# Two loads of v moved from SyncE's queue to ScalarE's, in sparse attention with a max-out layer behind it

## The chip, the cores and the metric

The kernel runs on one core of one Trainium2 chip. The metric is the device time of one execution in microseconds. The engines are TensorE (PE), VectorE (DVE), ScalarE (ACT), GpSimd (POOL) and SyncE (SP, which here only issues transfers). The 16 DMA engines of the core move the data; loads are issued from SP's queue (q1 in the profile), the stores of the output mostly from ScalarE's (q10).

## The reference

Two stages. The first is attention over 4 batches, 8 heads, 768 positions of 64 elements: each position sees the positions less than 16 away, and a summary of every block of 32 positions. The summary of k is the block's maximum, that of v its mean.

```
k_sum = k.reshape(B, H, nb, block, D).max(axis=3)          # block 32, nb 24
v_sum = v.reshape(B, H, nb, block, D).mean(axis=3)
scores_l = where(|i - j| < 16, scale * q @ k.T, -1e9)
scores_s = scale * q @ k_sum.T + log(32)
a = softmax(concat([scores_l, scores_s]))
x = (a @ concat([v, v_sum]))          # heads side by side: 3072 tokens x 512
```

The second stage is a feed-forward layer of 1,024 hidden units that takes the larger of two products:

```
out = maximum(x @ w1, x @ w2) @ w_out
```

## The kernel before

**Tiling.** The work on attention goes by batch b (0 to 3) and by pair of heads hp (0 to 3). In the text k12 is k of batch 1, pair 2; likewise q and v. k and q of a pair are loaded in 32-bit floats (384 KB each, `load_kq`, L358), cast to 16 bits (`prep`, L515), turned by TensorE (or, in some pairs of later batches, by a DMA) and placed in SBUF; the block maxima of k are put beside k. v of a pair is loaded by `load_v` (L371, also 384 KB, in 1,536 pieces of 256 B), cast by `cast_v` (L384) and spread by `spread_v` (L392): copies to the odd tiles, block sums by TensorE (L432), and copies of the sums. `scores` (L582) multiplies q and k, with an exponential on ScalarE (L625) behind it; `values` (L635) multiplies by v, VectorE divides (L659, L661), and the result is turned (L674) into xt.

The max-out layer uses max(a, b) = a + max(b - a, 0). `load_w12` (L688) loads w1 and w2 in two halves each (four loads of 1 MB) and makes the difference wd (L700, two on GpSimd and two on VectorE). `load_wo` (L724) loads w_out, `make_w1o` (L733) computes w1 times w_out, so that the layer is x (w1 w_out) + max(x wd, 0) w_out. `maxout` (L749) makes the hidden products (L757), the Relu (L762) and the output (L778, L785).

**Order of the work.** Every piece of work is handed to a planner (`Plan`, L113) as a task with an engine, an estimated duration, the buffers it reads and writes, and a priority. The planner simulates the engines and fixes one order of all tasks, by its own estimates; `run` (L155) then calls the tasks' functions in that order, which issues the instructions. On the chip each engine works through its instructions strictly in that order and waits by semaphores for what it needs. In the planned order SP issues, in batch 0: k00, q00, v00, k01, q01, v01, k02, q02, k03, q03, v02, v03, then the four weight loads, then q10, k10, v10, k11, q11 and the two loads of w_out. ScalarE has: cast k00, cast q00, two small copies of k00, cast v00, exp of pair 0 (first part), place k01, exp of pair 0 (second part), the odd copies of v01 and its sums, cast k03, two small copies of k01, place q03, exp of pair 1, cast v03 and so on. On GpSimd stand cast q01, cast q02, cast q03, the copies of the sums of v01, cast v02. The cast of v00 is planned directly behind the load of q03 in the overall order.

**Buffers and semaphores.** There are four buffers for loaded v (`vfr`, L247), six for k and q, four for weights, so that w_out needs buffers that the first halves of w1 and w2 held. The loads take eight completion semaphores in turn, and the issue of a load waits until the earlier load with the same semaphore has landed. With the order given above, v02 shares a semaphore with v00, and v03 with k01.

**Fillers.** `stay_busy` (L823) puts 40 tasks of two products of zeros (L830) among TensorE's first work, where it would otherwise be idle.

Of the kernel before, what the change touches and what calls it, by code (L numbers as in the profile page):

```python
# [16 lines left out]
ACT = mybir.ActivationFunctionType  # L17
# [64 lines left out]
class Task:  # L82
    done, start = 1e9, None
# [29 lines left out]
class Plan:  # L113
# [9 lines left out]
    def op(self, engine, us, fn, read=(), write=(), change=(), touch=(), behind=(), prio=0.0, label="", port=False):  # L123
        t = Task()
        t.engine, t.us, t.fn, t.label = engine, us, fn, label
        t.port = engine == "POOL" or port and engine == "DVE"
        t.prio = (prio + CFG["bump"].get(label, 0), len(self.tasks))
        t.new, t.behind = [*write, *change], behind
        t.deps = {w for b in (*read, *change) for w in b.writers}
        for b in t.new:  # L130
            b.writers.append(t)
        for b in (*read, *touch, *t.new):
            b.users.append(t)
        self.tasks.append(t)
        return t
# [57 lines left out]
def kernel(  # L193
# [14 lines left out]
    nc = tc.nc  # L208
    B, H, S, D = 4, 8, 768, 64
# [10 lines left out]
    op = plan.op  # L220
# [39 lines left out]
    vx = [Buf(vxr) for _ in range(B)]  # L260
# [109 lines left out]

    def load_v(b, hp, prio):  # L371
        f = vin[b, hp] = Buf(vfr)
        op("SP", 1.9, lambda: nc.sync.dma_start(  # L373
            out=f.ap[:].rearrange("p h m d -> p (h m) d"),
            in_=v[b, 2 * hp:2 * hp + 2].rearrange("h (m r) d -> r (h m) d", r=128)),
           write=[f], prio=prio, label=f"load v{b}{hp}")

    def by_parity(b):
        return vx[b].ap[:].rearrange("p (m w) h c -> p w m h c", w=2)

    vin, mains = {}, {}
    ready = {(b, hp): Buf(Ring([None])) for b in range(B) for hp in range(NP)}

    def cast_v(b, hp, engine, prio):  # L384

        f, done = vin[b, hp], Buf(Ring([None]))
        mains[b, hp] = done
        copy(engine, {"D": 0.6, "A": 0.85, "P": 0.8}, lambda: (
            by_parity(b)[:, 0, :, 2 * hp:2 * hp + 2, 0:D].rearrange("p m h d -> p h m d"), f.ap[:]),
             read=[f], write=[vx[b], done, ready[b, hp]], prio=prio, label=f"cast v{b}{hp}")  # L390

    def spread_v(b, h0, h1, prio, engines):  # L392

# [91 lines left out]
    def copy(engine, us, aps, label, port=True, halves=False, **kw):  # L485
        engine = ENG[engine]
        us = us if isinstance(us, float) else us[engine[0]]
        def fn():
            for o, i in [aps(0), aps(1)] if halves else [aps()]:
                {"DVE": nc.vector.tensor_copy, "ACT": nc.scalar.copy,  # L490
                 "POOL": nc.gpsimd.tensor_copy}[engine](out=o, in_=i)
        op(engine, us, fn, label=label, port=port, **kw)
# [354 lines left out]
    for hp in range(NP):  # L847
        load_kq(0, hp, hp)
        load_v(0, hp, CFG["kv"][hp])
        cast_v(0, hp, CFG["vc"][hp], CFG["kv"][hp])  # L850
        spread_v(0, 2 * hp, 2 * hp + 2, CFG["kv"][hp] + CFG["sp"], (CFG["od"][hp], CFG["se"][hp], CFG["sr"][hp]))
# [5 lines left out]
    for b in range(1, B):  # L857
        for hp in range(NP):
            at = 1000 * b + 20 * hp - CFG["ld"]
            load_kq(b, hp, at)  # L860
            load_v(b, hp, at + 10)
            cast_v(b, hp, CFG["lvc"][4 * b - 4 + hp], at + 10)
        spread_v(b, 0, H, at + 11, (CFG["lod"][b - 1], CFG["lse"][b - 1], CFG["lsr"][b - 1]))
        attention(b, 1000 * b)
# [37 lines left out]
```

## Time and profile before

| what | value |
|---|---|
| three runs | 172.28, 170.13, 171.58 us; median 171.58 |
| the profiled execution | 172.63 us, of which the span of the trace is 170.9 us |
| instructions | 4,532 |
| mean granted TensorE clock | 0.999 |
| read from HBM, written | 25.17 MB, 6.29 MB |
| DMA, mean over the span | 210 GB/s |
| q1 (SP's loads and turns), q10 (ScalarE's stores) | 73.1% and 10.6% of the 16 engines' time |

The largest shares of the chain of work that ended last are TensorE 64%, DMA 13%, the SP queue 10% and VectorE 8%. In a timeline, each row has the start, the duration, the engine (a q behind it marks an instruction that its sequencer handles, such as the issue of a DMA), the line, the operation, what it writes and reads, and in brackets the idle time ahead of it with what ended it. Rows of the same kind that follow each other are merged and carry their number (x3). Casts and copies that one helper issues all stand under L490. Times are microseconds from the start of the span.

### The profile page before, as it was taken

Reading aid. Unit: us, or ns where it says so; the run is one execution under the profiler, and the core shown is the slowest. Engines: PE = TensorE matmul, PEld = TensorE weight load, DVE = VectorE, ACT = ScalarE, POOL = GpSimd, SP = SyncE. Lnnn points to the kernel's source line nnn. Section 1 sums busy time; section 2 is a strip of 40 time slices with the busy share of each in tenths; the row PEclk is TensorE's granted clock in tenths of the full one; section 3 lists DMA queues with packets and bytes.
Section 4 is the critical chain, followed back from the end, with each engine's and each line's share of the span. In section 5 each row is a group of like instructions: output and inputs, shape, how many; then the busy total and the mean of one; then the engine's idle time right before and its main releaser. Section 6 shows DMA issues by size and latency. Waiting matters only on the chain.

```text
span 170.9 us, 4532 instructions
## 1 busy us (share of the span) xinstructions
PE 159.0 (93%) x1859; PEld 106.5 (62%) x1859; DVE 105.7 (62%) x224; ACT 93.0 (54%) x146; POOL 42.2 (25%) x73
## 2 busy tenths in 40 slices
PE   4885598999899999999999999999999999999992
PEld 4765366998546555568475675775746658756662
DVE  6778999899678998547996562929628460000001
ACT  3667485486963456626167476491665706523420
POOL 7713789340227041009200201104110000000000
PEclk9999999999999999999999999999999999999999
DMA  5999799999999999998499999993864617011113
GB/s 176 307 310 282 186 395 380 332 320 360 274 315 227 218 307 317 229 190 231 90 223 333 261 273 174 252 158 74 190 151 112 145 35 184 4 61 62 61 61 123
DMA packets 69396, 35.82 MB, mean 210 GB/s; under 512 B 56576, under 2 KB 63360, under 8 KB 69376
## 3 DMA queue, kind: packets, MB, share of 16 engines
q1 hardware_dynamic: 65856, 29.38, 73.1%
q10 hardware_dynamic: 3520, 6.16, 10.6%
q8 instruction: 14, 0.23, 0.6%
q14 instruction: 6, 0.05, 0.1%
HBM read 25.17 MB, written 6.29 MB: 184 GB/s over the span
## 4 chain that ended last, share of the span: by engine, by line
PE 64%; DMA 13%; SPq 10%; DVE 8%; issue 2%; POOL 1%; DVEq 0%; POOLq 0%
PE banks L785 22%; PE banks L757 19%; PE banks L778 10%; DMA wf<-in_moe_w_dram 8%; DMA wf<-in_moe_w_out_dram 5%; SPq L367 5%; PE banks L741 4%; PE banks L648 3%; SPq L373 3%; DVE vx L490 3%; PE banks L600 3%; SPq L693 3%; PE banks L543 1%; DVE ks L562 1%; DVE qx L490 1%
## 5 line engine op out<-in xcount | busy, mean ns | idle before, releaser
L785 PE MATMUL banks<-wo,g 128*128 128x512 bf16 (+2 forms) x208 | 46.9, 363 | 0.0
L757 PE MATMUL banks<-xt,wd 128*128 128x256 bf16 x384 | 46.4, 273 | 0.0
L757 PEld LDWEIGHTS <-wd 128*128 128x128 bf16 x384 | 36.7, 98 | 6.5 <-issue 0.2
L762 ACT ACTIVATE g<-banks 128x512 bf16<-128x512 f32 x48 | 27.8, 602 | 13.7 <-PE banks L757 13.5
L794 ACT COPY o<-banks 128x512 f32<-128x512 f32 x23 | 13.5, 587 | 32.4 <-PE banks L785 30.8
L785 PEld LDWEIGHTS <-g 128*128 128x128 bf16 x208 | 18.4, 98 | 17.7 <-issue 0.2
L778 PE MATMUL banks<-w1o,xt 128*128 128x512 bf16 (+2 forms) x104 | 23.7, 363 | 0.0
L490 POOL CAST kqb<-kqf 128x768 bf16<-128x768 f32 x12 | 11.6, 968 | 37.1 <-PE banks L543 17.4
L625 ACT ACTIVATE pba<-banks 128x1024 bf16<-128x1024 f32 x16 | 16.4, 1025 | 6.2 <-PE banks L600 5.7
L632 DVE TENSOR_TENSOR pba<-pba,mask 128x1024 bf16<-128x1024 bf16 x12 | 8.5, 711 | 14.1 <-ACT pba L625 14.1
L490 DVE COPY o<-banks 128x128 f32<-128x128 f32 x2 | 0.6, 292 | 26.8 <-PE banks L785 26.8
L661 DVE TENSOR_TENSOR xs<-banks,inv 128x512 bf16<-128x512 f32 x24 | 16.3, 687 | 0.6
L562 DVE TENSOR_REDUCE ks<-kx 128x24 bf16<-128x768 bf16 x16 | 15.0, 945 | 1.3 <-DMA kx<-kqb 1.2
L778 PEld LDWEIGHTS <-xt 128*128 128x128 bf16 x104 | 9.8, 98 | 8.8
L490 POOL CAST vx<-vf 128x768 bf16<-128x768 f32 x7 | 6.2, 889 | 23.4 <-DMA vf<-in_v_dram 23.3
L600 PEld LDWEIGHTS <-kx 64*128 64x128 bf16 x416 | 7.3, 96 | 6.7 <-issue 5.7
L490 ACT CAST kqb<-kqf 128x768 bf16<-128x768 f32 x9 | 7.9, 880 | 5.6 <-DMA kqf<-in_k_dram 2.7
L625 ACT ACTIVATE pbb<-banks 128x512 bf16<-128x512 f32 x16 | 9.7, 604 | 0.9 <-ACT o L794 0.9
L830 PE MATMUL banks<-zeros 128*128 128x128 bf16 x80 | 8.5, 259 | 1.8 <-DVE zeros L826 1.8
L490 POOL COPY kx<-kx 128x32 bf16<-128x32 bf16 (+1 forms) x12 | 5.5, 462 | 18.3 <-DMA kx<-kqb 12.1
L490 DVE COPY vx<-vx 64x3168 bf16<-64x3168 bf16 (+5 forms) x15 | 9.3, 632 | 0.2
L600 PE MATMUL banks<-qx,kx 64*128 64x64 bf16 (+2 forms) x416 | 9.4, 190 | 0.0
(85 smaller groups left out, 188.3 us busy)
## 6 DMA issues: line engine op xcount, KB each, us to landing
kqf<-in_k_dram SPq DMA_DIRECT2D x16, 384.0 KB, 6.7
kqf<-in_q_dram SPq DMA_DIRECT2D x16, 384.0 KB, 5.8
vf<-in_v_dram SPq DMA_DIRECT2D x16, 384.0 KB, 7.5
out_dram<-o ACTq DMA_DIRECT2D x19, 256.0 KB, 3.2
wf<-in_moe_w_dram SPq DMA_DIRECT2D x4, 1024.0 KB, 9.6
wf<-in_moe_w_out_dram SPq DMA_DIRECT2D x2, 1024.0 KB, 9.3
out_dram<-o ACTq DMA_DIRECT2D x4, 224.0 KB, 3.2
vx<-sums SPq DMA_DIRECT2D x4, 99.0 KB, 3.3
```

Of the source, the lines that this page charges most:

```text
L367: op("SP", (1.2, 1.13)[n], lambda f=f, src=src: nc.sync.dma_start(out=f.ap[:], in_=src[b, 2 * hp:2 * hp + 2].rearrange("h (p j) d -> p h ( ...
L490: {"DVE": nc.vector.tensor_copy, "ACT": nc.scalar.copy, "POOL": nc.gpsimd.tensor_copy}[engine](out=o, in_=i)
L562: op("DVE", 0.95, lambda: nc.vector.tensor_reduce(out=ks.ap[:], in_=free(kt(), 128, [256, NM], [192, 2], [32, 2], [1, 32]), axis=AX.X, op= ...
L600: nc.tensor.matmul(out=bank(ps[i], 1024)[:, 512 * a + at + n0:512 * a + at + n1], lhsT=kx[b, hp].ap[r, 128 * t + 128:128 * t + 256], rhs=q ...
L625: op("ACT", (1.03, 0.6)[i], lambda: nc.scalar.activation(out=pv(), in_=bank(ps, 1024).rearrange("p (a c) -> p a c", a=2)[:, :, 0:64 * n], ...
L632: op("DVE", (0.69, 0.43)[i], lambda: nc.vector.tensor_tensor(out=pv(), in0=pv(), in1=m, op=ALU.mult), read=[mask_in], change=[pb], prio=pr ...
L661: op("DVE", 0.69, lambda: nc.vector.tensor_tensor(out=x.ap[:], in0=av()[:, :, :, 0:D], in1=inv.ap[:].to_broadcast([128, 2, 4, D]), op=ALU. ...
L757: nc.tensor.matmul(out=bank(ps)[:, 256 * s:256 * s + 256], lhsT=wd[n].ap[:, c, 128 * s:128 * s + 128], rhs=x.ap[:, c, :], start=(c == 0), ...
L762: op("ACT", 0.6, lambda n=n, ps=ps: nc.scalar.activation(out=g.ap[:, 2 * n:2 * n + 2, :].rearrange("p f n -> p (f n)"), in_=bank(ps), func ...
L778: nc.tensor.matmul(out=bank(ps, c1 - c0), lhsT=x.ap[:, c, sl], rhs=w1o[c].ap[:, cols], start=(c == 0), stop=False)
L785: nc.tensor.matmul(out=bank(ps, c1 - c0), lhsT=g.ap[:, f, sl], rhs=wo[f // 2].ap[:, f % 2, cols], start=False, stop=(f == FC - 1))
L794: nc.scalar.copy(out=aps()[0], in_=aps()[1])
```

## The change

The loads of v02 and v03 (third and fourth pair of batch 0) are no longer issued by SP. Their tasks stay in the plan as SP tasks with the same duration, buffers and priority, so that the planned order is unchanged, but their function does nothing; the load itself is kept in a list, `later_v`. The cast of v00, which ran on ScalarE before and stays there, issues both kept loads on ScalarE's queue right after its own instruction.

```
     def load_v(b, hp, prio):
         f = vin[b, hp] = Buf(vfr)
-        op("SP", 1.9, lambda: nc.sync.dma_start(
-            out=f.ap[:].rearrange("p h m d -> p (h m) d"),
-            in_=v[b, 2 * hp:2 * hp + 2].rearrange("h (m r) d -> r (h m) d", r=128)),
+
+        def load(queue):
+            queue.dma_start(out=f.ap[:].rearrange("p h m d -> p (h m) d"),
+                            in_=v[b, 2 * hp:2 * hp + 2].rearrange("h (m r) d -> r (h m) d", r=128))
+
+        if b == 0 and hp >= 2:
+            later_v.append(load)
+        op("SP", 1.9, (lambda: None) if b == 0 and hp >= 2 else lambda: load(nc.sync),
            write=[f], prio=prio, label=f"load v{b}{hp}")
...
     def cast_v(b, hp, engine, prio):
...
+        def cast_then_load():
+            nc.scalar.copy(out=aps()[0], in_=aps()[1])
+            for load in later_v:
+                load(nc.scalar)
+
+        done_by = dict(read=[f], write=[vx[b], done, ready[b, hp]], prio=prio, label=f"cast v{b}{hp}")
+        if (b, hp) == (0, 0):
+            op("ACT", 0.85, cast_then_load, port=True, **done_by)
+            return
+        copy(engine, {"D": 0.6, "A": 0.85, "P": 0.8}, aps, **done_by)
```

The instructions of the loads are the same as before; the issuing engine and the place in the order differ. Since the kept loads are issued where the cast of v00 stands in the overall order, directly behind the load of q03, they take the same two semaphores as before.

More of the change, by code (lines that the diff above doesn't have):

```diff
@@ L379, in by_parity @@
         return vx[b].ap[:].rearrange("p (m w) h c -> p w m h c", w=2)
-    vin, mains = {}, {}
+    vin, mains, later_v = {}, {}, []
     ready = {(b, hp): Buf(Ring([None])) for b in range(B) for hp in range(NP)}
@@ L387, in cast_v, with aps @@
         mains[b, hp] = done
-        copy(engine, {"D": 0.6, "A": 0.85, "P": 0.8}, lambda: (
-            by_parity(b)[:, 0, :, 2 * hp:2 * hp + 2, 0:D].rearrange("p m h d -> p h m d"), f.ap[:]),
-             read=[f], write=[vx[b], done, ready[b, hp]], prio=prio, label=f"cast v{b}{hp}")
+        def aps():
+            return by_parity(b)[:, 0, :, 2 * hp:2 * hp + 2, 0:D].rearrange("p m h d -> p h m d"), f.ap[:]
+        def cast_then_load():
[7 more added lines that the diff above has]
+        copy(engine, {"D": 0.6, "A": 0.85, "P": 0.8}, aps, **done_by)
     def spread_v(b, h0, h1, prio, engines):
```

## The prediction

> **What bounds the kernel now.** I read the page first (busy times, slices), then the timelines of SP, ScalarE, GpSimd and TensorE over the first 45 us, then a table by windows. A load is called by its kind, batch and head pair: q03 is q of batch 0, pair 3.
>
> ```profile
> PE 159.0 (93%) x1859; PEld 106.5 (62%) x1859; DVE 105.7 (62%) x224; ACT 93.0 (54%) x146; POOL 42.2 (25%) x73
> ...
> PE   4885598999899999999999999999999999999992
> ...
> DMA  5999799999999999998499999993864617011113
> ```
>
> TensorE is busy in nearly every slice from the eighth on (a slice is 4.27 us, so from 30 us). The order of its instructions is fixed, so the rest of the span is a block of work about 140 us long, and whatever shifts its start shifts the end. The change acts in the 30 us before it. There the DMA engines are the busiest (nines from the second slice, one 7 in the fifth).
>
> ```profile
> 8.34 0.89 SPq L367 DMA_DIRECT2D kqf<-in_q_dram  x1
> 9.34 0.58 SPq L367 DMA_DIRECT2D kqf<-in_k_dram  x1
> 10.02 0.41 SPq L367 DMA_DIRECT2D kqf<-in_q_dram  x1
> 10.49 4.17 SPq L373 DMA_DIRECT2D vf<-in_v_dram  x2
> 14.70 5.47 SPq L693 DMA_DIRECT2D wf<-in_moe_w_dram  x4
> ```
>
> SP's issues: q02, k03, q03, then v02 and v03 in 4.17 us (0.46 and 3.65 in the trace), then the four weight loads. [...]
>
> ```profile
> 14.12 1.28 POOL L490 CAST kqb<-kqf 128x768 bf16<-128x768 f32 x1 [3.03 <-DMA kqf<-in_q_dram]
> 17.80 0.83 POOL L490 CAST kqb<-kqf 128x768 bf16<-128x768 f32 x1 [2.39 <-DMA kqf<-in_q_dram]
> 18.69 1.74 POOL L490 COPY vx<-sums 32x792 bf16<-32x792 bf16 x2
> 20.50 0.83 POOL L490 CAST vx<-vf 128x768 bf16<-128x768 f32 x1
> 22.00 1.92 POOL L490 COPY vx<-vx 64x768 bf16<-64x768 bf16 x3 [0.67 <-ACT vx L490]
> 23.97 1.75 POOL L490 COPY vx<-sums 32x792 bf16<-32x792 bf16 x2
> 25.78 1.04 POOL L490 CAST w1b<-wf 128x1024 bf16<-128x1024 f32 x1
> 26.79 4.67 POOL L700 TENSOR_TENSOR wd<-wf,wf 128x1024 bf16<-128x1024 f32 x2
> ```
>
> GpSimd is the reading that carries the forecast. It waits for q02 (until 14.12) and q03 (until 17.80), and from then to 31.46 it is almost without a gap. The cast of v02 (20.50) does not wait for a DMA: it stands in order behind the cast of q03 and the sums. So what is late in this front is q03, not v02.
>
> ```profile
> 12.89 0.83 PE L830 MATMUL banks<-zeros 128*128 128x128 bf16 x12
> ...
> 15.46 0.51 PE L543 MATMUL banks<-identity,kqb 128*128 128x128 bf16 x6 [1.74 <-POOL kqb L490]
> ...
> 18.68 0.51 PE L543 MATMUL banks<-identity,kqb 128*128 128x128 bf16 x6 [1.37 <-POOL kqb L490]
> ...
> 31.52 1.05 PE L757 MATMUL banks<-xt,wd 128*128 128x256 bf16 x8
> ...
> 43.81 2.75 PE L741 MATMUL banks<-wo,w1t 128*128 128x512 bf16 x12 [0.58 <-POOL wo L490]
> ```
>
> TensorE waits for the same two casts (1.74 and 1.37 us). Its turn of q03 at 18.68 stands ahead of the scores of pair 1 (19.03), so the exps wait too: ScalarE sits 2.24 us before placing q03 at 19.23. The block starts at 31.52, right after GpSimd's second wd. Later there is one gap, 0.58 us, for w_out.
>
> ```profile
> 14.50:17.00 2.50, 1.53 (x22) 1.53 (x23) 1.99 (x4) 1.64 (x3) 0.91 (x1) 1.00 1.27 244
> ...
> 17.50:19.00 1.50, 0.32 (x6) 0.32 (x7) 1.50 (x3) 0.00 (x0) 1.14 (x2) 1.00 0.29 55
> ```
>
> The last two columns are the DMA share and GB/s. While v02 and v03 move, the engines are full at 244 GB/s; then they run nearly dry (0.29), since the weights are issued too late.
>
> **The change part by part.** *Removed from SP:* 0.46 + 3.65 us of issue and two gaps of 0.05, 4.2 us in all. The first weight load is issued at about 10.5 instead of 14.70. What this is worth is bounded by the dry stretch: 0.71 x 1.5 us, with 0.20 x 0.5 from 17.0 and 0.15 x 1.0 to 20.0 (shares 0.80 and 0.85 there), 1.3 us. But the weights' landings are set by the engine that is last: v03 lands at 20.17 in the trace and the first weight, whole, at 22.95, 2.8 us later, about as far as the second is behind the first (25.65). So on the last engine there is no hole, and I take 0. Nor is anybody waiting: GpSimd comes to w1b at 25.78 straight from its sums, VectorE waits 0.25 us for the fourth weight at 32.66, TensorE under 0.1 for the third at 29.90. Gain taken: 0; bounds 0 and -1.3. SP's later loads (q10, k10) then wait for their buffers, not behind v.
>
> *Added to ScalarE:* two issues. By the v rows on SP one is 0.46 us; ScalarE's own stores are 0.34 to 0.43. v02 goes out with or just behind the cast (7.26 to 8.09). v03's issue in the trace carries a wait for the semaphore that k01's landing raises (loads use eight in turn); k01 lands at 9.10, so the issue ends about 9.6. Next on ScalarE is the exp at 9.75, which today waits 1.66 us for TensorE: the cover is there, cost 0. Upper end: v03 held as long as on SP, 3.65, to about 12.8; exp, place k01 and the odd copies come 3 us late. VectorE's max of k01 (13.29) then slips about 1.4 us, and ScalarE's idle 0.46 and 0.85 and the wait for k03 take the rest. I take 0, as the nearest row, an issue on an empty queue, is 0.47 (the v load at 1.83).
>
> *Moved past the others:* this is the term that counts. Today q02, k03 and q03 are ahead of v02 and v03. On ScalarE's queue v02 goes out before q02 (8.34) and v03 begins at 9.1, before k03 (9.34). The engines are full (share 1.26 from 8 to 10 us, 1.06 from 10 to 13.5), so what is let in ahead pushes the others back. A v load is 393 KB; at 244 GB/s that is 1.6 us. Lower end 0, if the engines first finish what SP has queued: ScalarE's 256 KB stores land after 2.0 us on idle engines (164.83), yet one issued at 62.06 into full ones took 7.1. Upper end 3.2, both loads ahead of q03. I take v02 in full, as a queue that starts empty hands over its 1,536 pieces at once, and a quarter of v03, whose pieces must queue behind v02's while k03 and q03 come in: 2.0 us for q03, 1.6 for q02. v01 (cast at 11.94, today waiting 0.25) may slip up to 1.6 too, beside q02's delay and not on top of it.
> [...]
>
> *What follows of a late q03:* GpSimd's cast, TensorE's turn and ScalarE's place wait for it and nothing after them to 31.46 has slack on GpSimd, so the start of TensorE's block moves by 2.0. Given back is the 0.58 us gap at 43.81: w_out is issued at 34.03 after the second wd, which moves from 31.46 to 33.5, still before 34.03. Sum: 0 + 0 + 2.0 - 0.6 = +1.4 us. The profiled execution took 172.63 (span 170.9 plus 1.7 outside it) and would take 174.0; it stands 1.05 above the median of the three runs, 171.58, so the median comes to 173.0.
>
> **The rivals.**
> *Not slower: the new queue is served last.* If the engines finish SP's k and q first, as the store of 62.06 suggests, q03 keeps 17.80 and v02 and v03 fill the dry stretch. Nothing waits for v before 20.5. Then VectorE's 0.25 and the 0.58 gap are all that can go: 171.6 - 0.6 = 171.0. It decides when fewer than 0.6 us of v passes q03. Against it: full engines at 8 to 9 us have only v01 and k02 queued, so v02 needs little patience to be ahead of q02.
>
> *Slower by more: TensorE falls back to its slow rate.* In the first 9 us its rows are slow: ten fillers in 1.27 us at 7.04 against twelve in 0.83 at 12.89; 16 scores in 0.61 at 9.10 against 0.41 at 19.55; two hide products 1.06 against 0.59; a turn of q 0.85 at 6.40 against 0.51. Today's longest wait is 1.74 us and no row after it is slow. With q02 1.6 us later the wait grows to 3.3 or 3.4. If that is too long, the turn of q03 and the first scores cost 0.34 + 0.47 + 0.20 = 1.0 more, and each further pair 1.0 more while it lasts, 3.1 at most; with 2.0: 173.0 + 2.0 = 175.0. For it: the idle time nearly doubles. Against: the granted clock reads 1.00 in every window, the slow first ones too, so it cannot tell.
> [...]
>
> [...]
>
> **How the numbers follow.** Forecast 0.42 (own range 172.2 to 174.0); served last 0.22 (171.0, from 170.3); slow rate 0.22 (175.0, to 177); both ahead 0.14 (174.2). Time 173.0. The range reaches to 170.7, past the case of no delay, and to 175.8, within the slow-rate case: 170.7 to 175.8 leaves out the far ends of the two, about 2 in 10. A measurement of this kernel can tell about 2% from no change, 3.4 us: slower by more is over 175.0, half of the slow-rate case and the upper part of the others with a slow rate on top, 0.23; faster by more, under 168.2, no case reaches: 0.03; within, 0.74.
>
> **What would show it.** The cast of q03 on GpSimd (17.80) at about 19.8 and the one of q02 (14.12) at 15.7; the first weight load issued near 10.5; v02 and v03 landed well before 18.8 and 20.2; the exp at 9.75 in place; the window 17.5 to 19 with a DMA share near 1; the hidden products at 33.5 instead of 31.52; the gap at 43.8 gone. Wrong it is if q03's cast stays near 17.8 (then served last), if the turn of q03 takes 0.85 (slow rate), or if ScalarE's exp moves past 12 (its issue was held).

## The result, and the profile after

The changed kernel takes 180.11 us (median of 6 runs, 179.08 to 183.2) against 171.47 for the kernel before (6 runs): 1.049 times as long, 95% interval 1.043 to 1.055, without two executions of the changed kernel (182.6 and 183.2) that ran in a slower state. The forecast was 173.0 with a range up to 175.8: the direction is right, the size is missed by a factor of six. The profiled execution after took 180.15, span 178.4.

The page of the changed kernel, busy times and slices (a slice is 4.46 us):

```profile
PE 161.7 (91%) x1859; PEld 107.6 (60%) x1859; DVE 105.0 (59%) x224; ACT 93.0 (52%) x146; POOL 41.1 (23%) x73
...
PE   4887715999999999799999999999999999999992
...
PEclk9999965699999999999999999999999999999999
DMA  5999999919999998794859999996773516101213
```

TensorE's long block is as before, but starts behind a new hole: 1 and 5 in the sixth and seventh slice, 22 to 31 us, with the granted clock at 6, 5 and 6 in the sixth to eighth. The DMA engines have no hole there; they are full up to the eighth slice.

ScalarE's cast of v03 in the kernel before, and then ScalarE's timeline of the changed kernel:

```profile
21.03 0.83 ACT L490 CAST vx<-vf 128x768 bf16<-128x768 f32 x1
```

```profile
7.40 0.83 ACT L397 CAST vx<-vf 128x768 bf16<-128x768 f32 x1
8.38 3.28 ACTq L375 DMA_DIRECT2D vf<-in_v_dram  x2
11.71 1.02 ACT L640 ACTIVATE pba<-banks 128x1024 bf16<-128x1024 f32 x1 [3.49 <-PE banks L615]
...
18.84 0.80 ACT L505 COPY qx<-banks 128x768 bf16<-128x768 bf16 x1 [1.20 <-PE banks L558]
...
27.86 0.83 ACT L505 CAST vx<-vf 128x768 bf16<-128x768 f32 x1 [7.12 <-DMA vf<-in_v_dram]
```

The last row is the result. The cast of v03 stood at 21.03 and waited for nothing; now it waits 7.12 us for its own load. v03 is issued at 11.28 (the second half of the 3.28 us row) and lands at 27.84. Before, issued at 11.00 by SP, it landed at 20.17. v02 lands at 18.13 (18.81 before).

GpSimd and TensorE of the changed kernel:

```profile
17.41 0.83 POOL L505 CAST kqb<-kqf 128x768 bf16<-128x768 f32 x1 [3.00 <-DMA kqf<-in_q_dram]
...
20.17 0.82 POOL L505 CAST vx<-vf 128x768 bf16<-128x768 f32 x1
28.82 1.83 POOL L505 COPY vx<-vx 64x768 bf16<-64x768 bf16 x3 [7.83 <-ACT vx L505]
...
33.52 4.66 POOL L715 TENSOR_TENSOR wd<-wf,wf 128x1024 bf16<-128x1024 f32 x2
```

```profile
28.74 0.80 PE L447 MATMUL banks<-vx,amean 128*128 128x128 bf16 x6 [5.94 <-ACT vx L505]
29.65 1.01 PE L606 MATMUL banks<-hide,identity 128*128 128x512 bf16 x2
...
39.07 1.05 PE L772 MATMUL banks<-xt,wd 128*128 128x256 bf16 x8
...
50.71 2.76 PE L756 MATMUL banks<-wo,w1t 128*128 128x512 bf16 x12
```

q03 is cast at 17.41, not later than the 17.80 of before. Yet q03 was held up. The traces hold 16 landing reports for each load, as many as there are DMA engines, and they are read here as one of each; the cast of q03 started 0.15 us behind the last of them (17.80 behind 17.65 before, 17.41 behind 17.26 in the changed kernel). By these reports the median engine (half of them earlier, half later) had q03 at 16.56 us against 14.69 before: 1.9 us later, close to the forecast's 2.0. But in the profiled execution before the last engine came 3.0 us behind the median (17.65), in the changed one 0.7 (17.26); in e11 below, which has the loads of before, the last one came at 15.54. So the cast of q03 hides the delay only against a late execution of before. What sets the time is another wait: both engines wait for the cast of v03, 7.83 and 5.94 us, and TensorE then runs at a lower rate for a while (granted clock 0.50 from 24.07 to 34.31 us, hide products 1.01 us instead of 0.59). The gap ahead of the row at 50.71 is gone.

The sum, on the two spans: the cast of v03 starts 6.83 us later (27.86 against 21.03); from there to the first hidden product it takes 0.72 longer (39.07 against 31.52, 7.55 in all); from there to w1 times w_out 0.65 shorter, the closed gap (11.64 against 12.29); from there to the end 0.60 longer (nearly all of it one wait of TensorE for VectorE's xs, 0.99 us at 73.52 against 0.37 at 65.98 before). That is 7.5, the difference of the spans 178.4 and 170.9. The profiled execution of before was 1.16 over its median, so the medians differ by 8.6.

A table by windows of the changed kernel, last columns granted clock, DMA share, GB/s:

```profile
11.50:13.50 2.00, 1.23 (x21) 1.02 (x19) 1.72 (x4) 1.79 (x3) 0.00 (x0) 1.00 1.24 288
...
16.00:25.50 9.50, 4.58 (x85) 3.16 (x86) 7.67 (x15) 3.51 (x6) 3.40 (x4) 0.92 1.08 356
25.50:28.00 2.50, 0.00 (x0) 0.00 (x0) 0.00 (x0) 0.14 (x1) 0.00 (x0) 0.50 1.05 369
```

From 16 to 25.5 us the DMA engines move 356 GB/s and v03 still does not arrive. The packet records show what moves: in each half microsecond from 16.5 to 25.5 us SP's queue starts 73 to 80 pieces of 2 KB (weights) and ScalarE's queue 75 to 84 pieces of 256 B (v). In this stretch the two queues start about the same number of pieces, though one kind is eight times as long: 315 GB/s of weights beside 40 of v. One piece of each takes 0.5 us x 16 / 78 = 103 ns on an engine, so by estimate the 96 short pieces of v03 for each engine (1,536 / 16) need 9.8 us. In the records v03's pieces start from 16.08 to 27.17 us, 1,487 of them before 25.5. Before, on SP's queue with little beside them, 2,035 pieces of v started from 14.5 to 17.0 us, which makes 1.9 us for a load.

The counts are not equal throughout: from 14.0 to 15.5 us SP's queue starts 98 to 117 pieces of 1,536 B per half microsecond beside 20 to 32 of v. And v02's pieces began at 11.69 us, and 1,174 of the 1,536 had started before the first piece of k03 (13.28 us), though k03 had been issued at 8.64; before the first of q03 (14.86) it was 1,468. So v02 did pass k03 and q03 for the most part, as the forecast has it. Why its first pieces went through together the traces do not show.

### The profile page after: what moved, and what is told of

Same layout as the page of the kernel before. It is cut to its first block, busy times and chain, and to the rows that moved or that the text cites. A ratio compares the mean times of both kernels' runs of the same rounds, so it can differ in the third digit from the quotient of the medians.

```text
span 178.4 us, 4533 instructions
## 1 busy us (share of the span) xinstructions
PE 161.7 (91%) x1859; PEld 107.6 (60%) x1859; DVE 105.0 (59%) x224; ACT 93.0 (52%) x146; POOL 41.1 (23%) x73
## 3 DMA queue, kind: packets, MB, share of 16 engines
q1 hardware_dynamic: 62752, 28.59, 67.2%
## 4 chain that ended last, share of the span: by engine, by line
PE 73%; DMA 13%; DVE 8%; SPq 2%; issue 1%; ACT 1%; DVEq 0%
PE banks L772 23%; PE banks L800 21%; DMA vf<-in_v_dram 13%; PE banks L793 10%; PE banks L756 4%; PE banks L663 4%; PE banks L615 4%; DVE vx L505 3%; SPq L367 2%; PE banks L558 2%; PE banks L689 2%; PE banks L606 1%; PE banks L729 1%; DVE qx L505 1%; DVE ks L577 1%
## 5 line engine op out<-in xcount | busy, mean ns | idle before, releaser
L674 DVE RECIPROCAL inv<-banks 128x8 f32<-128x8 f32 x24 | 4.7, 199 | 14.1 <-PE banks L663 14.0
L615 PEld LDWEIGHTS <-kx 64*128 64x128 bf16 x416 | 7.8, 99 | 7.8 <-issue 6.5
L845 PE MATMUL banks<-zeros 128*128 128x128 bf16 x80 | 9.0, 261 | 2.6 <-DVE zeros L841 1.8
L615 PE MATMUL banks<-qx,kx 64*128 64x64 bf16 (+2 forms) x416 | 9.9, 195 | 0.0
```

What stands on the lines that cost most here:

```text
L615: nc.tensor.matmul(out=bank(ps[i], 1024)[:, 512 * a + at + n0:512 * a + at + n1], lhsT=kx[b, hp].ap[r, 128 * t + 128:128 * t + 256], rhs=q ...
L845: nc.tensor.matmul(out=bank(ps, 128), lhsT=zeros[:], rhs=zeros[:], start=True, stop=True)
```

## The experiments

Theory A is this sharing, put as a supposition: the engines take a piece from each queue in turn. Theory B: v03 is late because its issue was held to 11.28 and it is served in order of issue, behind two weight loads. Theory C: what costs is ScalarE itself, held for 3.3 us by its issues. The slow rate of TensorE is a fourth suspect.

| kernel | time, us | ratio to before, interval | v03 landed | cast of q03 | cast of v03 | first hidden product |
|---|---|---|---|---|---|---|
| before | 171.47 | | 20.17 | 17.80 | 21.03 | 31.52 |
| changed | 180.11 | 1.049, 1.043 to 1.055 | 27.84 | 17.41 | 27.86 | 39.07 |
| e3 v03 in long pieces | 173.43 | 1.012, 1.003 to 1.020 | 21.61 | 18.45 | 22.26 | 32.28 |
| e4 weights in short pieces | 175.48 | 1.022, 1.013 to 1.031 | 22.49 | 18.34 | 22.52 | 33.29 |
| e1 v02 alone moved | 172.70 | 1.008, 1.004 to 1.013 | 19.99 | 18.39 | 22.56 | 32.20 |
| e2 v03 alone moved | 173.35 | 1.013, 1.005 to 1.021 | 17.66 | 18.18 | 22.38 | 33.20 |
| e6 weights behind q10 | 176.62 | 1.033, 1.027 to 1.039 | 25.23 | 19.35 | 25.26 | 34.60 |
| e9 weights behind place q02 | 173.43 | 1.008, 1.004 to 1.012 | 20.74 | 18.99 | 23.16 | 32.91 |
| e7 both at the cast of q00 | 175.03 | 1.022, 1.017 to 1.028 | 18.96 | 20.29 | 23.65 | 33.37 |
| e10 v03 ahead of v02 | 181.68, one run | | 18.22 | 18.11 | 21.34 | 40.60 |
| e11 ScalarE held, loads as before | 171.07 | 0.996, 0.993 to 1.000 | 19.64 | 15.69 | 19.66 | 29.84 |
| e5 fillers, second time | 180.26 | 1.050, 1.044 to 1.057 | 28.59 | 18.44 | 28.61 | 39.18 |
| e8 v02 alone, fillers | 173.18 | 1.011, 1.007 to 1.015 | 20.10 | 18.45 | 21.68 | 31.95 |

Times are medians, starts and landings those of one profiled execution. Each ratio is to runs of the kernel before made in the same session (medians 171.15 to 172.27), so it is not the quotient with 171.47.

**e3: v03 in long pieces.**

```
+        if (b, hp) == (0, 3):       # in load_v's load(queue)
+            queue.dma_start(out=f.ap[:].rearrange("p h m d -> p h (m d)"),
+                            in_=v[b, 2 * hp:2 * hp + 2].rearrange("h (p j) d -> p h (j d)", j=J))
+            return
```

> As the changed kernel, but v03 is fetched in 256 pieces of 1,536 B instead of 1,536 of 256 B (the rows of v03 then stand in another order, so that part of the output is wrong); bytes, queue, place and semaphore stay. Theory A (the engines take one piece from each queue in turn, so that v03's 96 short pieces per engine go at the pace of the weights' 2 KB pieces): v03 has 16 pieces per engine instead of 96, goes through in about 3 us and lands near 15 instead of 27.84; ScalarE's cast of v03 no longer waits; time 171 to 173. Theory B (v03 is late because its issue is held to 11.28 and is then served in the order of issue, behind the two weight loads issued before it): it is still served behind 2 MB of weights, lands at 24 or later, time 176 or more. Theory C (ScalarE held 3.3 us by its two issues is what costs): no change, 180.

ScalarE's row in this run:

```profile
22.26 0.83 ACT L509 CAST vx<-vf 128x768 bf16<-128x768 f32 x1
```

No wait any more; v03 lands at 21.61 though issued at 11.84, and the time falls from 180.11 to 173.43. Same bytes, queue and place; the number of pieces is what was changed. It landed later than the 15 expected: v02, with its short pieces, is ahead of it in the queue and now lands at 19.20 itself. B, which had 176 or more, fails; C, which had 180, fails.

**e4: weights in short pieces.**

```
-                out=f.ap[:],
-                in_=w.rearrange("(c p) n -> p c n", p=128)[:, :, 512 * half:512 * half + 512]),
+                out=f.ap[:].rearrange("p c (x n) -> p (c x) n", n=128),
+                in_=bass.AP(w.tensor, w.offset + 512 * half, [[1024, 128], [24576, 16], [1, 128]])),
```

> As the changed kernel, but the four weight loads are made of 512 B pieces instead of 2 KB (same bytes, same place; the pieces are fetched from wrong places of w1 and w2, so the hidden products are wrong). Theory A: the other side of the sharing, each turn costs v03 a fourth as long, so v03 lands near 17 to 20 instead of 27.84 and the wait of ScalarE's cast falls from 7.1 us to under 1; the weights themselves become slower, time 172 to 176. Theory B: v03 stays behind the weights, lands at 27 or later, 180 or more. Theory C: 180.

The other side of the sharing: v03 lands at 22.49 instead of 27.84 with its own load untouched, 2.5 us outside the expected stretch but with the wait gone (cast at 22.52, straight behind other work). The weights are slower, the last lands at 34.44 instead of 30.63, and still the time falls to 175.48. The stretch was forecast too short because a turn was taken to cost a fourth: from 16.5 to 20.0 us the queues start 159 to 180 pieces of 512 B and 166 to 182 of 256 B per half microsecond, so a pair takes 47 ns against 103. The numbers are again equal. So they are in e3 (55 to 59 pieces on either queue from 16.5 to 18.5 us, nearly all of 2 KB and of 1,536 B) and in e9 below, where v03 goes beside k and q (88 to 98 pieces of 1,536 B and 90 to 105 of 256 B, 14.5 to 17.5 us). In these stretches A holds on both sides.

**e1 and e2: one load alone.**

```
-        if b == 0 and hp >= 2:
+        if b == 0 and hp == 2:      # e2: hp == 3; the same in the line of the SP task
```

> Only v02 goes to ScalarE's queue; v03 stays on SP, ahead of the weights. v02's issue waits for k01 as in the changed kernel. Theory A: v02 shares turns with k02 to q03 and with v03, not with the weights; both land before 20, ScalarE's cast of v03 does not wait; 170.5 to 172.5. Theory B: v03 is on SP, no longer held: 170.5 to 172.5 as well. Theory C: ScalarE is held for one issue alone, the same. The recorded prediction's own term (v02 pushes q03 back by 1.6) gives 172.5 with q03 cast at 19.4 on GpSimd.

> Only v03 goes to ScalarE's queue, at the place of the cast of v00; v02 stays on SP ahead of the weights. v03's issue then waits for k01 (8.4 to 9.1) and not for v01. Theory A: v03 shares turns with k03, q03 and v02 before the weights begin, so most of its pieces are through before 18; lands 18 to 20, time 170.5 to 172.5. Theory B: the hold is gone, lands near 14, 170.5 to 172.5. If the changed kernel's loss is in v03 being on ScalarE's queue at all, it shows here: 176 or more.

Either load alone costs about 1%: 172.70 and 173.35. In e2 v03, on ScalarE's queue, is the faster of the two: it lands at 17.66, sharing with k, q and v, and not with weights. So the queue is not slow by itself. Both came out over the expected 172.5 (and e3 over its 173). TensorE's rate fell in both: in e2 the waits for q02, k03 and q03 are 0.78, 0.92 and 1.68 us, and the turn of q03 takes 0.82 instead of 0.51. Whether that is what they lost, e8 asks below. The same in e1:

```profile
16.46 0.55 PE L558 MATMUL banks<-ident,kqb 128*128 128x128 f32 x3 [0.79 <-ACT kqb L505]
16.85 0.28 PE L845 MATMUL banks<-zeros 128*128 128x128 bf16 x2
19.27 0.82 PE L558 MATMUL banks<-identity,kqb 128*128 128x128 bf16 x6 [2.15 <-POOL kqb L505]
```

```profile
17.00:19.00 2.00, 0.12 (x3) 0.00 (x0) 1.85 (x6) 0.03 (x1) 0.61 (x1) 1.00 1.16 298
19.00:21.00 2.00, 1.73 (x14) 0.89 (x16) 0.00 (x0) 0.80 (x1) 1.88 (x3) 0.57 1.04 381
```

The granted clock falls, to 0.57 on the mean of these 2 us, at the end of a wait of 2.15 us; the trace's record of the clock puts the fall at 19.29. In the 3.6 us up to it TensorE had done two rows, 0.7 us. In the kernel before, from 10.21 us on, where its record begins, the longest wait was 1.74 and the clock stayed at 1.00. The length of a wait does not decide alone: in e2 the fall is at 18.50 us (0.87 on the mean of 17 to 19 us, 0.50 from 19 to 25), inside the wait of 1.68 us, which is shorter than the 1.74 of before. What decides, no run shows.

**e6 and e9: the weights held back.**

```
-            op("SP", 2.9, lambda f=f, w=w: nc.sync.dma_start(...
+            op("SP", 2.9, lambda f=f, w=w: later_w.append(lambda: nc.sync.dma_start(...
...
+                if (b, hp, n) == (1, 0, 1):        # behind the load of q10
+                    for load in later_w:
+                        load()
...
+    nc.vector.memset(first_w[0].ap[:, 0, 0:1], 0.0)   # e9 only, behind VectorE's place q02
```

> Both v loads on ScalarE's queue as in the changed kernel, but SP issues the four weight loads only behind the load of q10, which waits for the cast of k02, so from about 15 us on, as late as before the change. Theory A (pieces in turn): v02 and v03 share with k02 to q03 only, go on alone from about 15, and land by 19; the cast of v03 does not wait; q03 later by at most 64 turns of 17 ns, 1.1 us; time 172 to 174, the rest being TensorE's slow rate after a longer wait for q03. If v on ScalarE's queue were slow for another reason (its issue held, the queue itself), v03 lands after 24 and the time stays over 176.

> Again both v loads on ScalarE's queue with the weights held back, this time by a real wait: SP issues q10 and then the first weight load, whose buffer VectorE touches (one element per partition, overwritten by the load) behind its placing of q02, so from about 17 us on; in the run before, the weights went out from 11.2. Theory A (pieces in turn): v02 and v03 are through or nearly so when the weights begin; v03 lands at 17 to 19.5, the cast of v03 does not wait for it, and what is left is q03's delay of up to 1.1 us and the slow rate: 171.5 to 174. If v03 still lands after 24 with no weights beside it, ScalarE's queue is slow by itself and theory A is wrong.

e6 did not do what it was made for: q10's buffer was free early, and the weights went out from 11.23, 1.3 us later than in the changed kernel. v03, issued already at 9.53, still lands at 25.23, and the time is in between, 176.62. e9 has the same issue of v03 (9.45) and the weights from 17.70: v03 lands at 20.74, time 173.43. Between these two the weights' start is what differs, and it is worth 4.5 us of landing and 3.2 us of time. That settles B: an early issue does not help beside the weights, and in e3 and e4 v03 was issued as late as in the changed kernel (11.84 and 10.97) and came early all the same. ScalarE's rows of v03's cast, e6 and then e9:

```profile
25.26 0.83 ACT L512 CAST vx<-vf 128x768 bf16<-128x768 f32 x1 [1.64 <-DMA vf<-in_v_dram]
```

```profile
23.16 0.83 ACT L512 CAST vx<-vf 128x768 bf16<-128x768 f32 x1
```

**e10: v03 ahead of v02.**

```
-            for load in later_v:
+            for load in later_v[::-1]:
```

> The changed kernel with the two v loads in the other order on ScalarE's queue: v03 first, v02 second. Theory A: the second one shares its turns with the weights, whichever it is; v03 lands near 18 and v02 near 27, GpSimd's cast of v02 (20.17 today) waits about 7 us in place of ScalarE's cast of v03, and the time stays at 179 to 182. If v03's own place in memory or buffer were to blame, v03 would still be late.

```profile
28.09 0.82 POOL L505 CAST vx<-vf 128x768 bf16<-128x768 f32 x1 [7.30 <-DMA vf<-in_v_dram]
```

v03 lands at 18.22, v02 at 27.97, and GpSimd's cast of v02 waits in place of ScalarE's of v03. Whichever is second meets the weights. It was run once, 181.68.

**e11: the hold alone.**

```
+                nc.scalar.copy(out=held[:], in_=vin[0, 1].ap[:, 0, 0, 0:1])   # behind the cast of v00
```

> The kernel before, all loads on SP, with one added ScalarE copy of one element per partition of v01 behind the cast of v00: ScalarE is held until v01 has landed (11.9), as the second issue holds it in the changed kernel, and the exp planned at 9.75 starts near 12.2. Theory A: the hold is hidden by ScalarE's waits for k03 and q03; within 0.5% of before, 170.7 to 172.4. Theory C (the hold costs): 173 or more.

```profile
11.28 0.19 ACT L392 COPY held<-vf 128x1 f32<-128x1 f32 x1 [3.02 <-DMA vf<-in_v_dram]
11.37 1.02 ACT L634 ACTIVATE pba<-banks 128x1024 bf16<-128x1024 f32 x1
```

ScalarE is held nearly as long as in the changed kernel, the exp of 9.75 starts at 11.37, and the time is 171.07, 0.996 of before (0.993 to 1.000). C falls: the hold costs nothing.

**e7: both loads earlier.**

```
+            if (b, hp, n) == (0, 0, 1):      # behind the cast of q00, not of v00
+                op("ACT", 0.85, cast_then_load, port=True, read=[f], write=[src], ...
```

> Both v loads on ScalarE's queue right behind its cast of q00 (about 6 us) instead of its cast of v00, with semaphores that are free, so that neither issue waits. Theory A: with 192 short pieces per engine against 24 us of k, q and v pieces from SP they pass nearly whole ahead of k03 and q03, which come 1.5 to 2.7 us later (cast of q03 at 19.3 to 20.5), and are through before the weights begin, so v03 lands before 16 and nobody waits for it; time 173 to 176 with the slow rate. Theory B (only the held issue is to blame): 171 to 172.

```profile
16.79 0.83 POOL L503 CAST kqb<-kqf 128x768 bf16<-128x768 f32 x1 [6.08 <-DMA kqf<-in_q_dram]
20.29 0.83 POOL L503 CAST kqb<-kqf 128x768 bf16<-128x768 f32 x1 [2.68 <-DMA kqf<-in_q_dram]
```

Here the forecast's term can be seen by itself: q03 is cast 2.5 us later than before, q02 2.7 (on the median engine they land 3.7 and 3.5 us later, about two v loads of 1.9), nobody waits for v03 (landed 18.96), and the kernel takes 175.03.

**e5 and e8: fillers against the slow rate.**

```
+            if tag == "06":                  # e5, ahead of the sums of v03; e8: 36, ahead of the turn of q03
+                for _ in range(105):
+                    nc.tensor.matmul(out=bank(ps, 128), lhsT=zeros[:], rhs=zeros[:], start=True, stop=True)
```

> The changed kernel with 105 products of zeros (about 5.9 us at the fast rate) on TensorE ahead of the sums of v03, where it waits 5.9 us; nothing else differs. If part of the loss is TensorE's slow rate after that wait (hide products 1.01 to 1.06 us at 29.65 instead of 0.59), the granted clock stays at 1.00, the hidden products start about 0.7 to 1.2 us earlier than 39.07, and the time falls to 178.5 to 179.5. If the slow rate is without consequence, 180 as before. In either case the wait of the cast of v03 (7.1 us) stays, and with it most of the loss.

> The kernel with the changed loads and 105 products of zeros ahead of the sums of v03 once more, since v03 landed 3.1 us later in its first profile than in that of the changed kernel, which hides what the rate of TensorE is worth. With the clock at 1.00 the stretch from the start of ScalarE's cast of v03 to the first hidden product was 9.34 us there against 11.21 in the changed kernel. If the slow rate costs, that stretch is again 9 to 10 us and the time, for a landing of v03 near 28, is 178 to 179; if landing and time come out as in the first run (180 to 181), the fillers give back what they save by another delay, and the share of the slow rate stays unmeasured.

> Only v02 on ScalarE's queue, and 36 products of zeros (2.0 us) on TensorE ahead of the turn of q03, where it waits 2.15 us in the run with v02 alone and fell to half rate (granted clock 0.57 from 19 to 23 us, turn of q03 0.82 instead of 0.51). If the slow rate is what that run lost, the clock stays at 1.00 and the time is 0.7 to 1.5 us lower, 171.2 to 172, equal to before; if the later q03 (18.39 instead of 17.80 on GpSimd) is, 172.7 stays.

e5 took 180.74, and 180.26 the second time: nothing gained. TensorE in the second run:

```profile
25.41 6.03 PE L448 MATMUL banks<-zeros 128*128 128x128 bf16 x105
31.27 0.50 PE L450 MATMUL banks<-vx,amean 128*128 128x128 bf16 x6
...
39.18 1.05 PE L775 MATMUL banks<-xt,wd 128*128 128x256 bf16 x8
```

The fillers began late, at 25.41, and the sums behind them 1.8 us after the cast of v03 had ended (29.44), so they took back what they saved: from the sums to the first hidden product it is 7.9 us at a granted clock of 9 tenths or more against 10.3 in the changed kernel (28.74 to 39.07). The second hidden product needs GpSimd's second wd. In the changed kernel that wd is ready at 38.18 and the product starts at 40.18, 2.00 later; before it was 31.46 and 32.63, 1.17 later. The difference, 0.8 us, is what TensorE's lateness adds, so the slow rate is worth about 0.8 of the 7.5 us at most; it was not measured closer. e8 keeps the clock at 1.00 throughout and takes 173.18, no less than e1; in its trace the second hidden product starts only 0.25 us earlier (33.06 against 33.31). So the slow rate is not what e1 lost. The later q03 is what is left, which is argued, not tested.

No version of these beats the kernel before beyond the noise; e11, at 0.996, is the kernel before with a wait in it.

## Why the prediction was wrong

**The step that failed** is in "Moved past the others", with the bounds in "Removed from SP" beside it. A v load was priced at 1.6 us, 393 KB at 244 GB/s, wherever it stood; the weights set free earlier were given a gain of 0 to 1.3 us and no loss; and v03 was expected "well before" 20.2, since "Nothing waits for v before 20.5". The 244 GB/s were read off a stretch in which v had the engines nearly alone (521 of the 611 KB moved from 14.5 to 17.0 us were v's; at that pace a load takes 1.9 us). Beside 2 KB pieces v03's pieces of 256 B started one for one, 103 ns for a piece of each (73 to 80 and 75 to 84 per half microsecond), by estimate 9.8 us for its 96 on an engine. What v does to k and q was weighed; what the weights do to v was not asked. The records show how many pieces start in a stretch; in what order an engine serves single pieces they do not show.

**q03 later by 2.0:** right in size. The term's ground, that an empty queue hands over its 1,536 pieces at once, was the author's estimate, and no run shows it: v02 was issued at 8.38 and its pieces started from 11.69 to 16.07 us, 1,468 of them before the first of q03. On the median engine q03 landed 1.9 us later, and its cast came 1.7 us later than in e11 (17.41 against 15.69). That it did not come later than in the profile before is chance: there the last engine was late. In the changed kernel this delay is not seen in the time, because the cast of v03 comes later still. Where v03 does not set the time, q03 is cast at 18.99 (e9), 18.39 (e1) and 20.29 (e7). e9, the change without the weights beside v, costs 0.8%, or 1.4 us, which is the sum of the forecast; but it is another kernel, with v02 issued 1.3 us earlier, so the agreement proves little.

**What follows of a late q03:** one reading was wrong. The block does not start with GpSimd's second wd; the kernel's first hidden product reads the first wd alone, and in e1 it starts (32.20) before the second is done (32.89). The second product waits for the second wd, and before it came 1.17 us behind it against 0.42 in e1, so GpSimd had some slack.

**The gain from SP set free, 0:** right. The weights go out from 9.93 (forecast 10.5) and land 1.9 us earlier (last one 30.63 against 32.57), and nobody uses it. More than that: this early issue is what brought them beside v03.

**ScalarE's two issues, 0:** right in the cost, wrong in the reason. The two loads did not keep their semaphores, as the section on the change says they would: in the trace the semaphores go round to a weight load, v02, a weight load and v03 in turn, so that v02 has that of k01 and v03 that of v01. v03's issue therefore waits for v01 (11.26); the exp moved from 9.75 to 11.71. e11 shows that this is free.

**The gap at 43.81:** gone, as forecast, worth 0.65.

**The rivals.** The slow rate did come (clock 0.50 from 24.1 to 34.3 us), but in the wait for v03, and worth about 0.8 us at most. That the granted clock "cannot tell" was wrong: the record of it begins only at 10.2 us in the trace before, behind the slow first rows, and in the changed kernel it reads 0.50 beside hide products of 1.01 us. The case of both v loads ahead of q03, at 0.14, did not come: when q03's last piece started (16.62 us), 87 of v03's 1,536 pieces had. k03 and q03 have 32 pieces on each engine, the two v loads 192, so if theory A held there, only a part of v would pass. Counting pieces there would have led to the weights too. "Served last" named the right suspect, patience on ScalarE's queue, and drew the wrong conclusion, since it counted 20.5 as out of reach for v03.

## What to carry to other kernels

Before a load is moved to a second queue, count its pieces against those of the loads that will run beside it: here, from 16.5 to 25.5 us, the two queues started about equal numbers of pieces (73 to 80 of 2 KB and 75 to 84 of 256 B per half microsecond), and the short pieces moved their bytes at an eighth of the other's rate (40 against 315 GB/s). Ask this of the moved load itself, not only of those that it passes, and of what the freed queue will issue sooner. A bandwidth read off a stretch where a load ran alone is no price for it in company: a v load took 1.9 us in the one, and the pieces of v03 took 11.1 us to start (16.08 to 27.17) in the other. And a load is in when its last engine is: before the change the median engine had q03 at 14.69 us, the last one at 17.65, and the cast started at 17.80. Before a landing is compared between two traces, look at the median engine as well.

## What the runs showed of the hardware beyond what was expected

The clock fell at the end of a wait of 2.15 us (e1, at 19.29) and inside one of 1.68 (e2, at 18.50), not only in a long one such as the 5.94 of the changed kernel (22.80 to 28.74, with the fall at 24.07 and the rise at 34.31), while before a wait of 1.74 left it at 1.00. What sets the time of a fall no run tests. And the kernel before is less fixed than its profile looks: in e11, with the same loads on the same queue, q03 was cast at 15.69 rather than 17.80 and the first hidden product came at 29.84 rather than 31.52, with a span of 168.9; spans of the kernel before run from 168.4. Its last engine had q03 at 17.65 us in the one and 15.54 in the other, while the median engines differ by 0.1 (14.69 and 14.81). So a delay of 2 us is not to be read from the landings of two executions.
